# Decoding float64 weights on chip: two VectorE steps instead of three, in a kernel of linear attention and an expert layer

## The chip, the cores and the metric

One core of one Trainium2 chip runs the kernel. The metric is the device time of one execution in microseconds (us); the time of the kernel before is the median of three runs. The engines are TensorE (PE in the profile, with PEld for its weight loads), VectorE (DVE), ScalarE (ACT), GpSimd (POOL) and the DMA queue of SyncE (SP).

## What is computed

Linear attention over 8 batches of 8 heads, 576 tokens and 64 channels, followed by a layer with a SoLU (h times its softmax) and a normalisation. All inputs are drawn with numpy; the weights `w_in` and `w_out` of the second part reach the kernel as 64-bit floats, seen as pairs of 32-bit words.

```python
def phi(x):
    proj = np.einsum('bhsd,df->bhsf', x, w_phi)
    proj = proj - np.max(np.abs(proj), axis=-1, keepdims=True)
    return np.concatenate([np.exp(proj), np.exp(-proj)], axis=-1)
...
num = np.einsum('bhsf,bhfd->bhsd', q_p, kv)
den = np.einsum('bhsf,bhf->bhs', q_p, z)[..., None] + 1e-06
...
h = x @ w_in                               # 4608 x 512 times 512 x 1024
solu = h * softmax(h)
ln = (solu - mu) / np.sqrt(var + 1e-06) * g_ln
return (ln @ w_out).astype(np.float32)     # 4608 x 1024 times 1024 x 512
```

## The kernel before

**Staging.** Attention runs in 16 units (two per batch), each in two halves. A unit's keys are projected by TensorE (`kp`), VectorE takes each token's largest absolute value (`km`) and subtracts it (`ks`), ScalarE takes the exponentials (`ke`), and TensorE sums keys times values (`V`). The queries of the first three units go the same way (`qp`, `qm`, `qs`, transposes `qT` by TensorE, exponentials `qe`); later ones are turned by VectorE (`qt`, `qm4`, `qb`) and lessened by GpSimd (`qs`). TensorE multiplies the two (`qo`, or inside `V`), ScalarE takes the result out of PSUM (`qv`, `de`), VectorE and GpSimd divide (`dc`, `dv`), VectorE turns it (`xt`), and SyncE stores it to a scratch in DRAM (`xo`). The second part reads it back in 18 groups of two tiles of 128 tokens (`xi`), as products of a high and a low part in three matmuls each, with shared sums and differences (`as`, `xh`, `xl`, `h`, `kc`, `mx`), then the exponentials, the product, the centring, the turn through DRAM (`ex`, `u`, `cen`, `tb`, `bo`, `bi`), and the product with `w_out` (`o`).

**The weights.** `w_in` and `w_out` are loaded in eight pieces of 1 MB (`wl`, 0 to 3 of `w_in`, 4 to 7 of `w_out`), 128 partitions by 1024 numbers of two words. A number is decoded in four instructions: ScalarE multiplies the high word, taken as a 32-bit float, by 2^-112, which moves the exponent from the 64-bit to the 32-bit bias (`ws`, `w_rebias`); VectorE shifts it left by 3 (`wb` 0), puts the top three bits of the low word in (`wb` 1), and puts the sign back in, which the shift has pushed out (`wb` 2; all three in `w_bits`). In the profile they are `w<-wraw` on DVE and `wraw<-wraw` on ACT. ScalarE and GpSimd then make the high and low parts (`wh`, `wth`, `woh`; `wlo`, `wk`, `wtl`, `wol`); `W_IN_READY` holds the first product of the second part until all of `w_in` is there.

**What sets the order.** Every operation is registered with `op(...)`, with its engine, the operations that it comes after and the buffers that it takes and gives back; costs and priorities in the registration play no part at run time. The order is the list `SEQUENCE` of 2612 numbers, written out by hand: `Plan.order` walks it and gives each operation its buffer, and `InOrder` keeps each engine's instructions in that order. So an instruction that waits holds up all that stand behind it on its engine. The tag `h` of PSUM (two banks, 1024 columns) has one buffer, used by the second part for h; the tag `a` has six.

Of the kernel before, what the change touches and what calls it, by code (L numbers as in the profile page):

```python
# [8 lines left out]
F32 = mybir.dt.float32  # L9
F32R = mybir.dt.float32r  # L10
U32 = mybir.dt.uint32
# [7 lines left out]
DM, DF = 512, 1024  # L19
# [12 lines left out]
JOIN = 4  # L32
GROUPS = ((0, 4), (4, 1), (5, 4))
# [158 lines left out]
)  # L192


# [1121 lines left out]
```

## Time and profile before

| | |
|---|---|
| median of 3 runs | 658.42 us (657.59 to 659.11) |
| the profiled execution | 657.98 us |
| its span, from the first to the last instruction | 656.3 us |
| mean granted TensorE clock | 0.99 |
| busy, share of the span | PE 95%, DVE 75%, ACT 70%, POOL 66% |

The shares are averages over the span. The page also cuts the span into 40 slices, names the chain of work that ended last, and lists groups of instructions; a helper (`InOrder`) issues all of them, so that nearly every instruction has the same line, L274, and groups are told apart by the names of their tiles. A stretch of the trace can be asked for by itself: how busy each engine was, who waited for whom, and each instruction in order of time.

### The profile page before, as it was taken

Reading aid. Unit: us, or ns where it says so; the run is one execution under the profiler, and the core shown is the slowest. Engines: PE = TensorE matmul, PEld = TensorE weight load, DVE = VectorE, ACT = ScalarE, POOL = GpSimd, SP = SyncE. Lnnn points to the kernel's source line nnn. Section 1 sums busy time; section 2 is a strip of 40 time slices with the busy share of each in tenths; the row PEclk is TensorE's granted clock in tenths of the full one; section 3 lists DMA queues with packets and bytes.
Section 4 is the critical chain, followed back from the end, with each engine's and each line's share of the span. In section 5 each row is a group of like instructions: output and inputs, shape, how many; then the busy total and the mean of one; then the engine's idle time right before and its main releaser. Section 6 shows DMA issues by size and latency. Waiting matters only on the chain.

```text
span 656.3 us, 19000 instructions
## 1 busy us (share of the span) xinstructions
PE 625.5 (95%) x7558; PEld 528.0 (80%) x7558; DVE 489.6 (75%) x1003; ACT 458.8 (70%) x842; POOL 434.9 (66%) x468
## 2 busy tenths in 40 slices
PE   5879799999999999999999999999998999999998
PEld 4769687878887888888888887888886888778787
DVE  6999989778878778588786778998886773542740
ACT  3869689858875877478685666887783776465653
POOL 0468889788376875665967658748758556587642
PEclk9989899999999999999999999999998999999999
DMA  8955415472556553554545473646444443275432
GB/s 287 364 201 155 103 63 190 132 223 92 171 190 196 141 156 131 160 165 113 175 151 167 149 191 106 207 132 214 120 144 131 141 120 136 61 193 161 160 129 80
DMA packets 100200, 103.38 MB, mean 158 GB/s; under 512 B 50448, under 2 KB 73232, under 8 KB 99600
## 3 DMA queue, kind: packets, MB, share of 16 engines
q1 hardware_dynamic: 100112, 102.18, 50.5%
q8 instruction: 59, 0.97, 0.6%
q14 instruction: 29, 0.24, 0.1%
HBM read 64.92 MB, written 37.22 MB: 156 GB/s over the span
## 4 chain that ended last, share of the span: by engine, by line
PE 78%; DVE 9%; DMA 4%; POOL 3%; SPq 3%; issue 2%; ACT 1%; ACTq 0%; POOLq 0%; DVEq 0%
PE o L274 26%; PE U L274 12%; PE h L274 10%; PE kv L274 10%; PE num L274 10%; PE pjk L274 5%; PE pq L274 3%; SPq L274 3%; DVE w L274 2%; DVE m L274 2%; DMA wraw<-in_w_in 2%; DMA rv<-in_v 1%; DVE blk L274 1%; POOL w_out_l L274 1%; DVE ek L274 1%
## 5 line engine op out<-in xcount | busy, mean ns | idle before, releaser
L274 POOL TENSOR_TENSOR uls<-uTs,uhs 128x1024 fp32r<-128x1024 f32 x35 | 83.5, 2388 | 47.1 <-ACT uhs L274 31.3
L274 PE MATMUL o<-w_out_h,uhs 128*128 128x512 f32 x280 | 112.0, 400 | 0.0
L274 PE MATMUL o<-w_out_h,uls 128*128 128x512 f32 x280 | 109.4, 391 | 1.1 <-POOL uls L274 1.1
L274 PE MATMUL o<-w_out_l,uhs 128*128 128x512 f32 x280 | 109.3, 390 | 0.0
L274 ACT ACTIVATE ek<-ek 128x512 f32<-128x512 f32 (+1 forms) x160 | 90.8, 586 | 22.8 <-DVE ek L274 21.9
L274 ACT ACTIVATE fq<-fq 128x640 f32<-128x640 f32 (+1 forms) x104 | 69.8, 680 | 12.3 <-DVE fq L274 11.5
L274 PEld LDWEIGHTS num<-kvf,fq 128*64 128x64 f32 x2304 | 70.3, 138 | 9.4 <-issue 5.6
L274 PE MATMUL kv<-rv,ek 128*64 128x65 f32 x2048 | 77.5, 223 | 0.0
L274 PE MATMUL num<-kvf,fq 128*64 128x65 f32 x2304 | 74.8, 223 | 0.7 <-ACT fq L274 0.6
L274 PEld LDWEIGHTS kv<-rv,ek 128*64 128x64 f32 x2048 | 71.7, 139 | 0.7 <-issue 0.4
L274 POOL TENSOR_TENSOR al<-S,ah 128x512 fp32r<-128x512 f32 x36 | 47.9, 1331 | 32.6 <-ACT ah L274 28.0
L274 POOL TENSOR_TENSOR blk<-blk,m 128x1152 f32<-128x1152 f32 x26 | 55.5, 2136 | 20.8 <-DVE m L274 19.7
L274 POOL TENSOR_TENSOR y<-E,rc 128x512 f32<-128x512 f32 x64 | 43.4, 699 | 38.5 <-DVE rc L274 17.4
L274 ACT ACTIVATE eu<-h,nm 128x1024 f32<-128x1024 f32 x36 | 40.1, 1115 | 39.6 <-DVE nm L274 33.5
L274 DVE SCALAR_TENSOR_TENSOR eu<-h,eu 128x1024 f32<-128x1024 f32 x36 | 43.8, 1217 | 26.5 <-ACT eu L274 26.3
L274 PEld LDWEIGHTS o<-w_out_h,uls 128*128 128x128 f32 x280 | 52.6, 188 | 13.2 <-POOL uls L274 2.0
L274 PEld LDWEIGHTS o<-w_out_h,uhs 128*128 128x128 f32 x280 | 52.6, 188 | 12.5 <-issue 0.4
L274 PEld LDWEIGHTS o<-w_out_l,uhs 128*128 128x128 f32 x280 | 52.6, 188 | 10.4
L274 DVE TENSOR_REDUCE m<-pjk 128x4 f32<-128x512 f32 (+1 forms) x80 | 48.4, 620 | 10.4 <-PE pjk L274 10.0
L274 DVE STREAM_TRANSPOSE ub<-eu 128x1024 f32<-128x1024 f32 x35 | 43.1, 1230 | 17.3 <-ACT eu L274 5.7
L274 PE MATMUL pjk<-wph,rawk 64*128 64x128 f32 (+1 forms) x544 | 48.0, 292 | 5.0 <-DMA rawk<-in_k 2.0
L274 DVE TENSOR_TENSOR ek<-pjk,m 128x512 f32<-128x512 f32 (+1 forms) x80 | 48.9, 621 | 4.8 <-PE kv L274 3.9
(111 smaller groups left out, 1565.2 us busy)
## 6 DMA issues: line engine op xcount, KB each, us to landing
du<-ub SPq DMA_DIRECT2D x35, 512.0 KB, 3.0
uTs<-du SPq DMA_DIRECT2D x140, 128.0 KB, 3.0
dx<-y SPq DMA_DIRECT2D x32, 288.0 KB, 2.3
out<-os SPq DMA_DIRECT2D x35, 256.0 KB, 3.2
rv<-in_v SPq DMA_DIRECT2D x32, 264.0 KB, 3.9
rawk<-in_k SPq DMA_DIRECT2D x32, 256.0 KB, 4.0
xT<-dx SPq DMA_DIRECT2D x64, 128.0 KB, 3.6
rawq<-in_q SPq DMA_DIRECT2D x26, 288.0 KB, 3.3
```

The source lines that it names most:

```text
L274: return self.tc.keep_in_program_order(method(*args, **kwargs))
```

## The change

The decoding of a piece is three instructions instead of four. ScalarE multiplies by Prelu instead of Copy: a negative result is multiplied by another 2^32, which sets the bit of the exponent that a shift by 3 moves to the place of the sign. For the four pieces of `w_in` (`BY_PSUM`) the result goes to PSUM, into the one buffer of the tag `h`, instead of back to the loaded tile. VectorE's first step takes the top three bits of the low word, and needs only the load; the second shifts the rescaled word and joins the two. The sign step is gone. In the diff's names: `ws`, then `wb` and `wd` (w_in) or `wj` (w_out).

```diff
+BY_PSUM = (0, 1, 2, 3)
...
 SEQUENCE = (
-    128, 3, 129, 132, 133, 185, 188, 118, 130, 84, 95, 119, 23, 189, 131, 103, 122, 120, 86, 85, 91, 124, 24,
...
     def w_rebias(i):
 
-        hf = W["raw", i][:, :, 1].bitcast(F32)
-        nc.scalar.activation(out=hf, in_=hf, func=AF.Copy, scale=(-1.0 if i < 4 else 1.0) * 2.0**-112)
-
-    def w_bits(i, step, tag):
-        raw = W["raw", i]
-        lo, hi = raw[:, :, 0], raw[:, :, 1]
-        if step == 0:
-            W[i] = sb(tag, [P, DF], U32, f"w32_{i}")
-            nc.vector.tensor_scalar(out=W[i], in0=hi, scalar1=3, scalar2=None, op0=ALU.logical_shift_left)
-        elif step == 1:
-            nc.vector.scalar_tensor_tensor(
-                out=W[i], in0=lo, scalar=29, in1=W[i], op0=ALU.logical_shift_right, op1=ALU.bitwise_or
-            )
-        else:
-            nc.vector.scalar_tensor_tensor(
-                out=W[i], in0=hi, scalar=0x80000000, in1=W[i], op0=ALU.bitwise_and, op1=ALU.bitwise_or
-            )
+        hi = W["raw", i][:, :, 1].bitcast(F32)
+        W["hi", i] = hf = bank("h", [P, DF], "whi") if i in BY_PSUM else hi
+        nc.scalar.activation(
+            out=hf, in_=hi, func=AF.Prelu, scale=(-1.0 if i < 4 else 1.0) * 2.0**-112, alpha=2.0**32
+        )
+
+    def w_low_bits(i, tag):
+        W[i] = sb(tag, [P, DF], U32, f"w32_{i}")
+        nc.vector.tensor_scalar(
+            out=W[i], in0=W["raw", i][:, :, 0], scalar1=29, scalar2=None, op0=ALU.logical_shift_right
+        )
+
+    def w_join_bits(i):
+        nc.vector.scalar_tensor_tensor(
+            out=W[i], in0=W["hi", i].bitcast(U32), scalar=3, in1=W[i], op0=ALU.logical_shift_left, op1=ALU.bitwise_or
+        )
...
+    JOINED = [("wd", i) if i in BY_PSUM else ("wj", i, "wb") for i in range(8)]
...
         op(("wl", i), "sync", dma(8 * P * DF), z - 9, w_load, (i, None))
-        op(("ws", i), "scalar", 1055, z, w_rebias, (i,), [("wl", i)])
-        op(("wb", i, 0), "vector", 600, z, w_bits, (i, 0, w_tag[i]), [("ws", i)], [(w_tag[i], T)])
-        op(("wb", i, 1), "vector", 1135, z, w_bits, (i, 1, None), [("wb", i, 0)], tiles=[T])
-        op(("wb", i, 2), "vector", 1135, z, w_bits, (i, 2, None), [("wb", i, 1)], tiles=[T])
+        ps_ = i in BY_PSUM
+        op(("ws", i), "scalar", act(DF, True) if ps_ else 1055, z, w_rebias, (i,), [("wl", i)],
+           [("h", ("whi", i))] if ps_ else ())
+        op(("wb", i), "vector", 600, z, w_low_bits, (i, w_tag[i]), [("wl", i)], [(w_tag[i], T)])
+        op(("wd", i) if ps_ else ("wj", i, "wb"), "vector", 1135, z, w_join_bits, (i,), [("wb", i), ("ws", i)],
+           tiles=[T, ("whi", i)] if ps_ else [T])
```

The operations that came after the third step now come after the join (`JOINED`). The list `SEQUENCE` is new from end to end, with 2604 numbers. Translated into names, its beginning reads so:

- On VectorE the first decoding step stood behind 13 other instructions of the attention, and now stands behind 21. The order there was: first step of piece 3, of 1, second and third of 1, second of 3, first of 0, third of 3, second of 0, first of 2, third of 0, second of 2, third of 2, with other instructions between most of them. It is now: first step of 3, one subtraction, join 3, first step of 1, one reduction, join 1, three others, first step of 0, join 0, seven others, first step of 2, two others, join 2; much later the first step of 6, then both of 4, the first steps of 5 and 7, and the joins of 7, 6 and 5.
- On ScalarE the rescaling of piece 3 is third, with the exponentials of the first keys behind it; that of 1 stands behind the first unit's first queries, and that of 0 and 2 soon after.
- On GpSimd the first work on weights is the low part of piece 3 instead of a difference of piece 1.
- On SyncE the load of piece 1 stands four places later than before, and pieces 0 and 2 no longer directly behind each other.
- On TensorE the order of projections, transposes and products is nearly that of before, with swaps of neighbours. In the second part the second half of the first tile's h (`h` 1) mostly comes ahead of the fourth shared product (`u4`) now.

## Rows read from the trace of the kernel before

**Rows 1.** The page: busy time, share of the span and instructions of each engine; then TensorE's busy tenths and the granted clock in 40 equal slices of the span.
```profile
PE 625.5 (95%) x7558; PEld 528.0 (80%) x7558; DVE 489.6 (75%) x1003; ACT 458.8 (70%) x842; POOL 434.9 (66%) x468
...
PE   5879799999999999999999999999998999999998
...
PEclk9989899999999999999999999999998999999999
```

**Rows 2.** Busy time by stage: stretch and length, then busy us and instructions of PE, PEld, DVE, ACT and POOL, the granted clock, the DMA share and GB/s.
```profile
0.00:10.00 10.00, 6.20 (x52) 5.07 (x52) 4.05 (x8) 1.28 (x1) 1.25 (x9) 1.00 0.75 213
10.00:100.00 90.00, 74.18 (x1311) 63.51 (x1310) 84.81 (x125) 70.75 (x151) 60.53 (x42) 0.94 0.57 194
...
120.00:656.30 536.30, 526.24 (x5967) 443.46 (x5965) 381.13 (x831) 367.20 (x657) 354.45 (x402) 1.00 0.50 150
```

**Rows 3.** The same for the instructions that read or write the loaded words (`wraw`) alone: DVE, then ACT.
```profile
10.00:100.00 90.00, 36.53 (x24) 9.41 (x8) 0.94 0.57 194
```

**Rows 4.** The instructions on the tile `wraw`: ns at least, median and at most, first and last start in us, forms.
```profile
L274 DVE SCALAR_TENSOR_TENSOR w<-wraw,w x16: 1166/1222/3274, 18.3 to 91.9; 128x1024 uint32<-128x1024 uint32 x16
L274 ACT ACTIVATE wraw<-wraw x8: 1128/1168/1257, 11.4 to 66.7; 128x1024 f32<-128x1024 f32 x8
L274 DVE TENSOR_SCALAR w<-wraw x8: 677/1321/2405, 13.6 to 77.4; 128x1024 uint32<-128x1024 uint32 x8
```

**Rows 5.** Who TensorE waited for in the first 160 us: us in total, times, longest.
```profile
PE dT L274 <- DVE dq L274: 4.4, 3, 3.0
...
PE pjq L274 <- issue: 2.2, 1, 2.2
PE pjk L274 <- DMA rawk<-in_k: 2.0, 1, 2.0
...
PE pjk L274 <- DVE dq L274: 1.3, 1, 1.3
```

**Rows 6.** The chain of work that ended last, in order of time, in the first 200 us: start, us, what.
```profile
26.88 1.21 DVE w L274
...
42.05 1.96 PE pjk L274 x16
...
64.71 0.69 DVE m L274
...
78.69 0.90 PE dT L274 x3
79.59 2.69 PE U L274 x6
...
87.29 2.14 POOL blk L274
...
96.20 2.35 POOL w_out_l L274
```

**Rows 7.** VectorE's instructions in order of time, the decoding steps with two sources and one with one source: start, us, instruction, count.
```profile
25.75 2.35 DVE L274 SCALAR_TENSOR_TENSOR w<-wraw,w 128x1024 uint32<-128x1024 uint32 x2
...
28.62 2.40 DVE L274 TENSOR_SCALAR w<-wraw 128x1024 uint32<-128x1024 uint32 x1
30.95 2.29 DVE L274 SCALAR_TENSOR_TENSOR w<-wraw,w 128x1024 uint32<-128x1024 uint32 x1
...
34.36 1.96 DVE L274 SCALAR_TENSOR_TENSOR w<-wraw,w 128x1024 uint32<-128x1024 uint32 x1
...
39.35 2.05 DVE L274 SCALAR_TENSOR_TENSOR w<-wraw,w 128x1024 uint32<-128x1024 uint32 x1
...
67.35 2.37 DVE L274 SCALAR_TENSOR_TENSOR w<-wraw,w 128x1024 uint32<-128x1024 uint32 x1
...
70.67 3.27 DVE L274 SCALAR_TENSOR_TENSOR w<-wraw,w 128x1024 uint32<-128x1024 uint32 x1
...
75.06 1.77 DVE L274 SCALAR_TENSOR_TENSOR w<-wraw,w 128x1024 uint32<-128x1024 uint32 x1
```

**Rows 8.** GpSimd's instructions in order of time: start, us, instruction, count, in brackets the idle time before and what ended it.
```profile
21.06 2.19 POOL L274 TENSOR_TENSOR w<-w 128x512 f32<-128x512 f32 x1 [19.21 <-DVE w L274]
...
39.05 1.27 POOL L274 TENSOR_TENSOR w<-w 128x512 f32<-128x512 f32 x1
40.28 2.25 POOL L274 TENSOR_TENSOR w<-w,w 128x512 f32<-128x512 f32 x1
...
70.48 2.38 POOL L274 TENSOR_TENSOR wt_l<-w,wt_h 128x1024 fp32r<-128x1024 f32 x1 [1.85 <-ACT wt_h L274]
```

**Rows 9.** Groups of instructions of the first 120 us, shapes kept apart: count, busy us, mean ns, idle before and what ended it.
```profile
L274 DVE SCALAR_TENSOR_TENSOR w<-wraw,w 128x1024 uint32<-128x1024 uint32 x16 | 26.0, 1642 | 0.0
...
L274 DVE SCALAR_TENSOR_TENSOR eu<-h,eu 128x1024 f32<-128x1024 f32 x3 | 3.7, 1220 | 0.5 <-ACT eu L274 0.4
...
L274 ACT CAST wb_h<-w 128x1024 fp32r<-128x1024 f32 x2 | 2.1, 1044 | 1.3 <-DVE w L274 1.3
...
L274 ACT ACT_TABLE_LOAD x1 | 1.3, 1283 | 0.7 <-PEq L1306 0.7
```

**Rows 10.** Busy time by stage, columns as in rows 2, for two more stretches.
```profile
40.00:60.00 20.00, 18.71 (x375) 17.03 (x375) 19.21 (x32) 17.94 (x41) 15.84 (x13) 0.91 0.54 171
...
480.00:520.00 40.00, 37.18 (x540) 31.57 (x540) 30.24 (x67) 26.27 (x50) 26.74 (x28) 0.96 0.46 145
```

**Rows 11.** Who TensorE waited for behind 160 us: us in total, times, longest.
```profile
PE h L274 <- DVE nm L274: 3.7, 2, 2.8
```

More of the change, by code (lines that the diff above doesn't have):

```diff
@@ L485, in linear_attention_then_moe @@
         op(("wl", i), "sync", dma(8 * P * DF), z - 9, w_load, (i, None))
-        op(("ws", i), "scalar", 1055, z, w_rebias, (i,), [("wl", i)])
-        op(("wb", i, 0), "vector", 600, z, w_bits, (i, 0, w_tag[i]), [("ws", i)], [(w_tag[i], T)])
-        op(("wb", i, 1), "vector", 1135, z, w_bits, (i, 1, None), [("wb", i, 0)], tiles=[T])
-        op(("wb", i, 2), "vector", 1135, z, w_bits, (i, 2, None), [("wb", i, 1)], tiles=[T])
+        ps_ = i in BY_PSUM
[4 more added lines that the diff above has]
+           tiles=[T, ("whi", i)] if ps_ else [T])
         if i >= 4:
-            op(("wg", i), "scalar", 1260, z, w_gain, (i,), [("wb", i, 2), "gain"], tiles=[T])
+            op(("wg", i), "scalar", 1260, z, w_gain, (i,), [JOINED[i], "gain"], tiles=[T])
     for p in range(2):
@@ L494, in linear_attention_then_moe @@
         z = w_time[p + 2]
-        op(("wh", p), "scalar", 560, z, w_in_hi, (p, p), [("wb", p, 2)], tiles=[A])
+        op(("wh", p), "scalar", 560, z, w_in_hi, (p, p), [JOINED[p]], tiles=[A])
         op(("wlo", p), "gpsimd", 1225, z, w_in_lo, (p, p), [("wh", p)], tiles=[A])
-        op(("wh", p + 2), "scalar", 947, z, w_in_hi, (p, p + 2), [("wb", p + 2, 2)], tiles=[B_])
+        op(("wh", p + 2), "scalar", 947, z, w_in_hi, (p, p + 2), [JOINED[p + 2]], tiles=[B_])
         op(("wlo", p + 2), "gpsimd", 2303, z, w_in_lo, (p, p + 2), [("wh", p + 2)], tiles=[B_])
-        op(("wk", p, 0), "gpsimd", 1225, z + 1, w_comb, (p, 0), [("wb", p, 2)], tiles=[A])
+        op(("wk", p, 0), "gpsimd", 1225, z + 1, w_comb, (p, 0), [JOINED[p]], tiles=[A])
         op(("wk", p, 1), "gpsimd", 1225, z + 1, w_comb, (p, 1), [("wk", p, 0), ("wlo", p + 2)], tiles=[A, B_])
@@ L512, in linear_attention_then_moe @@
         first, second = 4 + 2 * ((i - 4) // 2), 5 + 2 * ((i - 4) // 2)
-        op(("woh", i), "scalar", 947, z, w_out_hi, (i,), [("wg", i), ("wb", first, 2)], tiles=[T])
-        op(("wol", i), "gpsimd", 2303, z, w_out_lo, (i,), [("woh", i), ("wb", second, 2)], tiles=[T])
+        op(("woh", i), "scalar", 947, z, w_out_hi, (i,), [("wg", i), JOINED[first]], tiles=[T])
+        op(("wol", i), "gpsimd", 2303, z, w_out_lo, (i,), [("woh", i), JOINED[second]], tiles=[T])
     def span(g):
```

272 rows, old and new, of the table SEQUENCE are left out of this document.

## The prediction

> **What bounds the kernel now.** I read the page first, then the same numbers cut into stages, then who TensorE waited for, then the chain that ended last, and at last the decoding instructions one by one. The reader should see four things.
>
> TensorE is the engine that ends last: it is busy 625.5 of 656.3 us, and its row of slices is full except at the start [rows 1]. The stages say where the other 30.8 us lie: from 120 us on it idles 10.1 us of 536, but between 10 and 100 us 15.8 us of 90 (90 - 74.18), and there the granted clock averages 0.94, which takes another 0.06 x 90 = 5.4 us of its work [rows 2]. So a change of the weights, which are decoded in this stretch alone, can win at most 15.8 + 5.4 = 21.2 us, and what comes later can only keep it or lose it.
>
> In the same stretch VectorE is busy 84.81 of 90 us [rows 2], and the 24 decoding instructions are 36.53 us of that [rows 3]. TensorE's waits name it: its transposes and projections wait 4.4 and 1.3 us for VectorE's subtraction `dq`; 2.0 us are a load of keys and 2.2 us nothing that the profile names [rows 5]. The chain goes the same way: from 26.88 to 42.05 us and from 64.71 to 78.69 us it is VectorE's queue, with decoding steps between the reductions that TensorE needs; from 87.29 to 98.55 us it is POOL [rows 6].
>
> The decoding steps have very different lengths: a step with two SBUF sources takes 1.17 us at least, 3.27 at most and 1.64 on average (26.0 us for 16, from the row of the page's first 120 us); the one-source step takes 0.68 to 2.41 us [rows 4, 9]. The long ones lie beside POOL's instructions: the step of 3.27 us at 70.67 beside one of POOL's from 70.48 [rows 7, 8]. POOL suffers too: the same 512-column subtraction takes 1.27 us alone and 2.19 or 2.25 us beside decoding steps [rows 8].
>
> **The change part by part.** The times are set against the profiled execution: 657.98 us, of which 656.3 are the span; it stands 0.44 us below the median of 658.42.
>
> *The third step goes.* Eight of 16 two-source steps vanish. Bare, that is worth 8 x 1.17 = 9.4 us of VectorE, at the mean 8 x 1.64 = 13.1 us. On the chain stand seven such steps: in the first stretch the second half of the pair at 25.75 (1.2) and those of 2.29, 1.96 and 2.05; in the second 2.37, 3.27 and 1.77 [rows 7]. They sum to 14.9 us, and half of that goes: **-7.5 us**. Bounds: 7 x 1.17 / 2 = -4.1 if only bare time is won, and -13.1 if all eight count. I take the middle value because it is read from the places where the chain ran.
>
> *The join of w_in reads PSUM.* Four of the eight remaining joins get one SBUF and one PSUM source. The trace has that form with the same 1024 columns: the product `eu<-h,eu` takes 1.22 us and hardly varies [rows 9]. Two such joins stand where the first stretch had steps averaging (1.2 + 2.29 + 1.96 + 2.05) / 4 = 1.88 us: 2 x 0.66 = **-1.3 us**; bounds 0 (no contention there any more anyway) and 4 x (1.64 - 1.22) = -1.7.
>
> The sources of the old steps are every second word, the PSUM source is dense. The rows show no price for the stride: 1.17 us at least with it, 1.22 in the dense form [rows 4, 9]. [...]
>
> *The rescaling.* Prelu in place of Copy, for w_in into PSUM. ScalarE's eight rescalings take 9.41 us together [rows 3], 1.17 us each [rows 4]; a dense 1024-column cast takes 1.04 us [rows 9]. 0 to -1.0 us of ScalarE, which is not the one that is late here (70.75 of 90 us [rows 2]): nothing. No row shows Prelu; the other functions share one table load in the whole span [rows 9]. If it doesn't, see the rivals.
>
> *The low word first.* The first step no longer waits for the rescaling, only for the load. VectorE had no idle time before any of these steps (the pieces follow without a gap [rows 7]), so nothing is won by itself: 0.
>
> *One PSUM buffer for four rescaled words.* The tag `h` has one slot. The rescaling of weight 1 waits for the join of weight 3, and by the new list only the first step of 1 and one reduction stand on VectorE between join 3 and join 1: 0.68 + 0.68 us against a rescaling of 1.17 us and two handovers. Behind that join waits all of VectorE, and behind the rescaling ScalarE's exponentials. I take **+0.5 us**; bounds 0 and 3 x 1.17 = +3.5 for three handovers. The list puts four and ten other instructions between the later joins, so the low end is nearer.
>
> *The clock.* TensorE's granted clock falls in this stage after it has waited for VectorE (its longest such wait is 3.0 us [rows 5]). If the first of these gaps closes, a part comes back: 40 to 60 us shows a granted 0.91, so 0.09 x 20 = 1.8 us [rows 10]; I take **-1.7 us**, bounds 0 and -5.4.
>
> *What is late next: POOL.* It begins its weights at 21.06 us [rows 8] and is busy 60.53 us between 10 and 100 [rows 2], so behind its start it has 90 - 11.1 - 60.5 = 18.4 us of idle time left to give. The new list puts weight 3 first, behind 21 reductions and subtractions of VectorE where 13 stood, so POOL starts no earlier. To end 8 us sooner it has to give up nearly half of its idle time. Bounds 0 and +8 (its chain at 87 us doesn't move at all); I take **+2.0 us**, nearer to the low end because its waits were for VectorE in the first place.
>
> *The new order of the rest.* TensorE's order of its products and of the attention changes only by swaps of neighbours; the second half of a tile's h now comes ahead of the fourth shared product. From 120 us on there are 10.1 us of idle time [rows 2], which can shrink or grow; I take 0.
>
> Sum: -7.5 - 1.3 + 0.5 - 1.7 + 2.0 = -8.0 us, so 657.98 - 8.0 = 650.0 for such an execution and **650.4 us** as a median.
>
> **The rivals.**
>
> *All of it arrives* (chance 0.15). The eight steps count at their mean, 13.1, and the four joins 1.7; less 0.5 that is 14.3, below the 21.2 - 2.0 - 2.2 = 17.0 us that TensorE can give back without its waits for keys and the nameless one. For it: VectorE is busy 94% of the stretch [rows 2]. Against it: between the two stretches of VectorE, from 42.05 to 64.71 us, the chain is TensorE's own work [rows 6], and an earlier start of it helps only as far as its inputs are there. Time 658.42 - 14.3 = 644.1.
>
> *POOL becomes the bound* (0.14). Its chain up to 98.55 us [rows 6] carries products and low parts that the change doesn't touch. Then only what POOL itself gains is left: two subtractions back from 2.19 and 2.25 to 1.27, 1.9 us. For it: 11.3 us of chain; against it: 18.4 us of idle time ahead of that. Time 656.5.
>
> *Slower: the new list opens gaps where TensorE is full* (0.12). The place is after 120 us, the mechanism a product of TensorE that stands too early behind VectorE's minimum `nm`. One such place exists: between 480 and 520 us TensorE stands still for 2.8 us [rows 11], and the stretch has a granted 0.96 over 40 us [rows 10], 1.6 us more: 4.4 us. One list trades such places for others; two more eat 8.8 us, so from the second on the gain is gone, and with three the time is 658.42 - 8.0 + 13.2 = 663.6. Against it: VectorE has slack there (381 of 536 us [rows 2]).
>
> *Slower too: Prelu needs another table* (0.03). The change then doesn't do what it says. Eight rescalings among exponentials mean up to 16 loads of 1.283 us [rows 9], 20.5 us of ScalarE, which with 70.75 [rows 2] would fill 91 us of the 82 that the forecast leaves for the stretch. The time lies between 650.4 + 9.3 and 650.4 + 20.5; I put 665. [...]
>
> **How the numbers follow.** The forecast has 0.56. The likeliest case reaches by its own bounds from 645 to 656. To hold 8 in 10 the range takes in most of the first rival and all of the second: 643.5 to 659.0, leaving out the slower rivals (0.15) and the lowest few. A measurement can tell about 0.2% from no change, 1.3 us here. Faster: the forecast (0.54 of its 0.56), the first rival 0.15 and half of the second, 0.08: 0.77. Same: 0.08. Slower: 0.15.
>
> **What would show it.** Right: 16 decoding instructions of some 20 to 24 us in all; joins of w_in at 1.2 us without long ones; TensorE's idle time between 10 and 100 us down by about 6 us; one table load. Wrong: TensorE's waits for `dq` replaced by equal ones for ScalarE or POOL (the PSUM slot, POOL's chain); more than 10 us of idle time after 120 us; more table loads. If the decoding shrinks as said but the first product of the expert network starts no earlier than at 79.59 us [rows 6], the step that took VectorE's saving for TensorE's was wrong.

## The result, and the profile after

The changed kernel takes 635.07 us, median of 4 runs (634.44 to 636.38), against 658.00 for the kernel before beside it: ratio 0.9657 [0.9629, 0.9685]. That is 15 us below the forecast of 650.4 and 8 below the low end of its range. The profiled execution took 634.97 us, its span 633.2.

The page of the kernel after: busy time by engine, TensorE's busy tenths, the granted clock, and the shares of the chain.

```profile
PE 617.8 (98%) x7558; PEld 525.0 (83%) x7558; DVE 475.3 (75%) x995; ACT 458.1 (72%) x842; POOL 432.0 (68%) x468
...
PE   6999899999999999999999999999999999999997
...
PEclk9999999999999999999999999999999999999999
...
PE 88%; DVE 6%; ACT 2%; DMA 2%; issue 1%; SPq 0%; ACTq 0%; DVEq 0%
```

TensorE idles 633.2 - 617.8 = 15.4 us instead of 30.8 [rows 1], and the row of the clock has no 8 left. (Read in steps of 1 us, the granted clock of the kernel before is 1.00 but for three places, 42 to 46, 76 to 84 and 499 to 504 us, each with 0.50 inside; a product of `h` takes 0.63 us at 501 us and 0.39 at 89 us. So its 0.96 between 480 and 520 us [rows 10] is a mean over a few us at 0.50 and the rest at 1.00. The kernel after has 1.00 in every such step.) The stages of the kernel after, with the columns of rows 2:

```profile
10.00:100.00 90.00, 83.83 (x1518) 72.43 (x1520) 83.78 (x142) 82.22 (x172) 69.55 (x50) 1.00 0.65 215
120.00:633.20 513.20, 508.24 (x5746) 430.86 (x5745) 371.54 (x810) 357.78 (x637) 345.36 (x394) 1.00 0.51 152
480.00:520.00 40.00, 39.40 (x571) 33.70 (x571) 34.56 (x77) 28.07 (x54) 26.31 (x33) 1.00 0.47 138
```

Between 10 and 100 us TensorE idles 6.2 us instead of 15.8, 9.6 us less, where the forecast's sign of being right asked for about 6. But behind 120 us it idles 5.0 us instead of 10.1 [rows 2], and the stretch from 480 to 520, where it stood still for 2.8 us at a granted 0.96 [rows 10], idles 0.6 us at 1.00 (the kernel after is at later work by then). VectorE is still busy 83.8 of the 90 us: a third step less did not make it idle, it made the stretch do more.

The decoding steps, first through PSUM, then the others; columns as in rows 4.

```profile
L274 ACT ACTIVATE whi<-wraw x4: 1074/1123/1131, 10.7 to 27.2; 128x1024 f32<-128x1024 f32 x4
L274 DVE SCALAR_TENSOR_TENSOR w<-whi,w x4: 1155/1219/1225, 18.4 to 32.6; 128x1024 uint32<-128x1024 uint32 x4
```

```profile
L274 DVE TENSOR_SCALAR w<-wraw x8: 682/1254/1739, 17.5 to 64.5; 128x1024 uint32<-128x1024 uint32 x8
...
L274 DVE SCALAR_TENSOR_TENSOR w<-wraw,w x4: 1714/1922/2106, 52.4 to 70.8; 128x1024 uint32<-128x1024 uint32 x4
```

The sums of the two, busy us of DVE and ACT between 10 and 100 us (the first row for the steps on loaded words, the second for those on PSUM):

```profile
10.00:100.00 90.00, 16.98 (x12) 9.30 (x8) 1.00 0.65 215
```

```profile
10.00:100.00 90.00, 4.82 (x4) 4.45 (x4) 1.00 0.65 215
```

16.98 + 4.82 = 21.8 us on VectorE against 36.53 [rows 3]; the forecast said 20 to 24. Who TensorE waits for, in the first 160 us and behind them:

```profile
PE pjq L274 <- DMA wph<-in_w_phi: 3.8, 1, 3.8
PE U L274 <- DVE blk L274: 2.2, 1, 2.2
PE h L274 <- DVE nm L274: 1.0, 1, 1.0
PE pjk L274 <- DMA rawk<-in_k: 0.9, 1, 0.9
PE pjq L274 <- DVE dq L274: 0.7, 1, 0.7
```

```profile
PE pq L274 <- DVE c L274: 0.6, 1, 0.6
PE pq L274 <- ACT os L274: 0.2, 1, 0.2
```

The 4.4 and 1.3 us for `dq` [rows 5] have shrunk to three waits of 0.4 to 0.7 us, a new wait of 2.2 us for VectorE's turn `blk` has come, and the 3.7 us for `nm` behind 160 us [rows 11] are gone altogether. One piece of the chain:

```profile
68.40 1.62 PE U L274 x6
```

The first product of the second part starts at 68.40 us instead of 79.59 [rows 6]. GpSimd's first work on weights starts at 22.09 us, 1 us later than before [rows 8]; there is one table load, 1.3 us, as in rows 9.

```profile
22.09 2.38 POOL L274 TENSOR_TENSOR wb_l<-w,wb_h 128x1024 fp32r<-128x1024 f32 x1 [20.24 <-DVE w L274]
```

```profile
L274 ACT ACT_TABLE_LOAD x1 | 1.3, 1283 | 0.7 <-PEq L1308 0.7
```

**A landmark.** To tell the head from the rest in every kernel, I use the first product with `w_out`: it needs the weights of both kinds and all of the first tile's chain. Its start is the first number behind the durations in the row of `o<-w_out_h,uhs`, here for the kernels before and after:

```profile
L274 PE MATMUL o<-w_out_h,uhs x280: 387/389/586, 115.8 to 649.3; 128*128 128x512 f32 x140
```

```profile
L274 PE MATMUL o<-w_out_h,uhs x280: 387/389/587, 102.2 to 626.3; 128*128 128x512 f32 x140
```

So the head took 115.8 us and takes 102.2, 13.6 less; from there to the end of the span it was 656.3 - 115.8 = 540.5 and is 633.2 - 102.2 = 531.0, 9.5 less. The landmark is not quite the same place in both: the new list has one projection of TensorE ahead of it (16 products of unit 4's keys, `kp` 2, some 1.1 us) that the old list has behind it. Counted on the same side the head wins 14.7 us and the rest 8.4. More than a third of the gain lies where the forecast put nothing.

### The profile page after: what moved, and what is told of

Its sections match the earlier page's. It is cut to its first block, busy times and chain, and to the rows that moved or that the text cites. A ratio compares the mean times of both kernels' runs of the same rounds, so it can differ in the third digit from the quotient of the medians.

```text
span 633.2 us, 19010 instructions
## 1 busy us (share of the span) xinstructions
PE 617.8 (98%) x7558; PEld 525.0 (83%) x7558; DVE 475.3 (75%) x995; ACT 458.1 (72%) x842; POOL 432.0 (68%) x468
## 4 chain that ended last, share of the span: by engine, by line
PE 88%; DVE 6%; ACT 2%; DMA 2%; issue 1%; SPq 0%; ACTq 0%; DVEq 0%
PE o L274 31%; PE U L274 15%; PE h L274 12%; PE num L274 10%; PE kv L274 9%; PE pjk L274 5%; PE pq L274 4%; DVE m L274 2%; DVE w L274 1%; DVE ek L274 1%; PE pjq L274 1%; DVE dq L274 1%; DMA xT<-dx 1%; ACT fq L274 1%; DMA out<-os 1%
## 5 line engine op out<-in xcount | busy, mean ns | idle before, releaser
L274 PEld LDWEIGHTS o<-w_out_h,uhs 128*128 128x128 f32 x280 | 52.6, 188 | 12.5 <-issue 0.2
L274 POOL TENSOR_TENSOR al<-S,ah 128x512 fp32r<-128x512 f32 x36 | 47.5, 1320 | 21.8 <-ACT ah L274 20.9
L274 DVE STREAM_TRANSPOSE ub<-eu 128x1024 f32<-128x1024 f32 x35 | 43.1, 1233 | 14.3 <-ACT eu L274 5.5
L274 DVE STREAM_TRANSPOSE blk<-pq 128x320 f32<-128x320 f32 (+1 forms) x104 | 43.4, 455 | 10.8 <-PE pq L274 10.7
L274 POOL TENSOR_TENSOR lq<-rawq,hq 128x576 fp32r<-128x576 f32 x26 | 37.2, 1432 | 20.9 <-ACT hq L274 20.1
```

What stands on the lines that cost most here:

```text
L274: return self.tc.keep_in_program_order(method(*args, **kwargs))
```

## The experiments

All with the landmark read in the same way from each kernel's own row. The ratio is to the kernel before on the same chip.

| kernel | median us | ratio, 95% | span | head | rest |
|---|---|---|---|---|---|
| before | 658.0 | | 656.3 | 115.8 | 540.5 |
| e1 new decoding, no PSUM, old list | 648.78 | 0.9867 [0.9841, 0.9893] | 648.9 | 108.1 | 540.8 |
| e2 old decoding, new list | 648.35 | 0.9878 [0.9845, 0.9910] | 645.7 | 114.5 | 531.2 |
| e3 new without PSUM | 638.43 | 0.9711 [0.9690, 0.9733] | 636.8 | 104.8 | 532.0 |
| e4 new head, old rest | 643.64 | 0.9790 [0.9769, 0.9812] | 641.7 | 102.2 | 539.5 |
| e5 e1 with the new rest | 642.67 | 0.9756 [0.9720, 0.9792] | 641.9 | 107.9 | 534.0 |
| e6 before, one join moved | 653.30 | 0.9929 [0.9902, 0.9955] | 651.9 | 116.2 | 535.7 |
| e7 before, clock held | 656.80 | 0.9980 [0.9964, 0.9997] | 653.4 | 115.4 | 538.0 |
| e8 e3, high word first | 640.21 | 0.9727 [0.9687, 0.9767] | 640.6 | 107.4 | 533.2 |
| e9 after, one stretch old | 644.92 | 0.9809 [0.9784, 0.9835] | 644.2 | 103.8 | 540.4 |
| e10 after, joins of w_in twice | 641.54 | 0.9751 [0.9725, 0.9777] | 641.6 | 108.3 | 533.3 |
| e11 after, joins of w_out twice | 642.89 | 0.9767 [0.9743, 0.9792] | 638.2 | 107.3 | 530.9 |
| e12 after, four operations moved | 638.05 | 0.9694 [0.9670, 0.9718] | 636.7 | 103.2 | 533.5 |
| e13 e4, one join moved | 640.81 | 0.9740 [0.9721, 0.9758] | 639.9 | 104.3 | 535.6 |
| e14 after, two more joins by PSUM | 635.67 | 0.9672 [0.9653, 0.9691] | 633.2 | 100.9 | 532.3 |
| e15 after, beside e13 and e14 | 635.80 | 0.9668 [0.9651, 0.9686] | 633.5 | 101.9 | 531.6 |

Kernels with one and the same list behind the head (e3, e8, e10, e11, e14, e15) show rests of 530.9 to 533.3, so a single span tells rests apart to some 2 us; the medians are the judge below that. The same holds for heads: the kernel after, e9 and e15 have one code and one order up to the landmark, and heads of 101.9 to 103.8. All kernels with the new list at their beginning (e2 to e4 and e8 to e15, and the kernel after) have the 1.1 us of projection in the head.

**Decoding and list apart: e1, e2, e3.** The names in the list stand for the numbers.

```diff
# e1: the list before
-BY_PSUM = (0, 1, 2, 3)
+BY_PSUM = ()
-SEQUENCE: new
+SEQUENCE: that of before, each join at the place of its second step, third steps struck
# e2: the kernel before, SEQUENCE new (three steps: the second and third at the place of the join)
# e3: only BY_PSUM = ()
```

> The kernel before, with its own list, but with two decoding steps: the join stands where the second step stood, the third is struck out, and the rescaled words of w_in stay in the loaded tile (the old list has no room for the PSUM buffer). Theory D (the decoding does it: VectorE's 14.7 us less decoding between 10 and 100 us bring back TensorE's idle time and the clock there, 14.9 us): 643 to 647 us. Theory O (the list does it; the two steps are worth only what the old chain shows, about 8 us, because the old list leaves no place for more): 648 to 654 us.

> The kernel before with its three decoding steps, in the new list: the second and third step stand one behind the other where the join stands. Theory D: VectorE gets its 14.7 us back, so the head is as late as before, and only what the list saves behind 100 us is left: 648 to 652 us. Theory O: the list keeps most of its gain: 637 to 644 us.

> The changed kernel with the rescaled words of w_in back in the loaded tile; list and two steps unchanged. Both theories: the four joins of w_in meet GpSimd again, 4 x (1.64 - 1.22) = 1.7 us of VectorE: 635 to 638 us. If the PSUM operand is the main thing, it is 640 us or more, with joins of 2 us and longer among those of w_in.

By the ratios each half alone is worth 8 to 9 us (e1 and e2), both together without PSUM 19 (e3), and with it 23. By the landmark the halves lie in different places: e1 shortens the head by 7.7 us and leaves the rest (540.5, 540.8); e2 leaves the head nearly alone (1.3 us) and shortens the rest by 9.3. The rest does not care how the weights were decoded. In the head, the new list is worth 1.3 us with the old decoding (115.8 to 114.5) and 3.3 with the new (e1 to e3, 108.1 to 104.8), each with 1.1 us more work of TensorE in it. What e1 waited for in its head and e3 and the kernel after don't (they have instead 2.2 us for `blk`):

```profile
PE U L271 <- POOL al L271: 1.8, 1, 1.8
PE h L271 <- DVE nm L271: 1.6, 2, 1.1
```

The order of the loads may be a part of it too. The chain of the kernel before [rows 6] begins with loads, up to 26.86 us, the longest a piece of `w_in`:

```profile
12.78 10.85 DMA wraw<-in_w_in
```

e7, with the old list, has that load on its chain as well (9.63 us); the chains of e2 and of the kernel after, with the new list, have no load of `w_in` or `w_out` ahead of the landmark. What this alone is worth no run tells.

e3 against the kernel after tells PSUM's share: 3.4 us by the medians, 3.6 by the ratios, whose intervals leave anything from 0.3 to 7. e3's four joins of w_in, from SBUF, on VectorE in order of time:

```profile
18.16 1.22 DVE L274 SCALAR_TENSOR_TENSOR w<-wraw,w 128x1024 uint32<-128x1024 uint32 x1
...
20.59 1.23 DVE L274 SCALAR_TENSOR_TENSOR w<-wraw,w 128x1024 uint32<-128x1024 uint32 x1
...
24.88 2.12 DVE L274 SCALAR_TENSOR_TENSOR w<-wraw,w 128x1024 uint32<-128x1024 uint32 x1
...
33.21 1.51 DVE L274 SCALAR_TENSOR_TENSOR w<-wraw,w 128x1024 uint32<-128x1024 uint32 x1
```

They sum to 6.08 us against 4.82 after: 1.26 us of VectorE, nearly the forecast's 1.3. The joins at 18.16 and 20.59, before GpSimd has work (21.84 us in e3), take as long from SBUF as from PSUM; only the two later ones are long. Beyond that, e3 has a granted clock of 0.98 between 10 and 100 us where the kernel after has 1.00, which is 0.02 x 90 = 1.8 us; the two make 3.1 of the 3.4. But that clock is not shown to be PSUM's: e13, whose joins do read PSUM, has the same lower clock in the same place, behind a wait of 2.1 us for `blk` where e3 has one of 2.2. From 70 to 80 us, first e3, then e13:

```profile
70.00:80.00 10.00, 10.00 (x42) 8.00 (x40) 7.92 (x15) 7.42 (x18) 9.82 (x8) 0.84 0.29 79
```

```profile
70.00:80.00 10.00, 10.00 (x44) 7.89 (x44) 7.86 (x16) 7.27 (x17) 9.85 (x7) 0.84 0.27 77
```

The kernel after has the same wait and 1.00 there.

**Where the list wins: e4, e5.** Spliced lists: the order of one list up to a point, and behind it what is left in the order of the other.

```diff
# e4: the kernel after
-SEQUENCE: new
+SEQUENCE: the first 500 places of the new one (about 100 us), the rest in the old order
# e5: e1
-SEQUENCE: old
+SEQUENCE: the first 888 places of the old one (about 205 us), the rest in the new order
```

> The changed kernel, whose list follows the new one for its first 500 operations (to about 100 us) and takes the rest in the order of the old list. Theory D and theory O both put about 15 us (idle time and clock) into the head; the rest of the new list then brings 23 - 15 = 8 us, and without it the time is 642 to 645 us. If the list behind the head is worth nothing by itself, and an earlier head alone closes the later gaps, it is 634 to 637 us.

> Two decoding steps without the PSUM buffer; the list follows the old one for its first 888 operations (to about 205 us) and the new one behind that. If what the new list saves behind the head is a thing of its own and adds up: 648.8 - 8.6 = 640 us, with TensorE's waits for nm behind 205 us gone. If the gaps behind the head come from a late head: 646 to 649 us.

e4 keeps the head to the tenth (102.2) and loses 8.5 us in the rest, 8.6 by the medians, which agrees with the 8.4 above; e5 keeps the head of e1 and wins 6.1 by the medians, 7.3 by the ratios, with the new order from 205 us on. So the list's gain is real, lies behind the head, and most of it behind 205 us.

**One operation: e6, e9, e13.** The 2.8 us of rows 11 are a wait of TensorE for the join `mx` 0 of group 11. In the list before it stands on VectorE behind reductions of unit 15, whose projections TensorE makes just before, and TensorE's next `h` stands behind the join.

```diff
# e6: the kernel before; e13: e4
+ ("moe", 11, "mx", 0)   directly behind ("moe", 11, "kc", 2), ahead of unit 15's reductions
- ("moe", 11, "mx", 0)   ahead of ("moe", 11, "h", 1)
# e9: the kernel after, its places 2060 to 2149 sorted into the order of the list before
```

> The kernel before with one operation of its list moved: the first minimum of group 11 (mx 0), at 498.7 us of VectorE, from behind the reductions of unit 15 to just behind the group's second kept sum, so that TensorE's product at 499.5 us no longer waits for it. If that wait is the list's own and drags the clock: -2.8 us for the wait and -1.7 to -3.6 us for the half-speed stretch behind it, 651 to 653.5 us. If the gap only moves on to the next wait: 656 to 658 us.

> The kernel after, with 90 of its 2604 places, those about group 11 near 470 to 490 us, put back into the order of the list before: the join of the first half of h (mx 0, which ends in the minimum nm) again stands on VectorE behind the two reductions of unit 15, whose projections TensorE makes just before, and the second half of h waits for it. Theory (one badly placed operation is most of what the list is worth behind the head): the wait of 2.8 us of rows 11 and the stretch of lower clock behind it (0.04 x 40 = 1.6 us, rows 10) return in the new list too: 635.1 + 4.4 = 639.5. Rival (the list's gain is spread over many small places, and 90 of 2604 places are worth little): 635 to 636. Rival (only the wait returns, without the clock): 637.9.

> The kernel with the new head and the old rest (643.6 us, 8.6 above the kernel after), with one operation of the rest moved: the join of the first half of group 11's h stands directly behind the third shared difference of its group on VectorE, ahead of the reductions of unit 15. Theory (one place holds most of it: a wait of 2.8 us and the lower clock behind it, as in the same move in the kernel before, which won 4.8): 643.6 - 4.8 = 638.8, and 3.8 us are left for all other places together. Rival (the old rest waits elsewhere once this wait is gone): 642 to 643.6. Rival (it is the whole): 635.

Moving that one operation wins (1 - 0.9929) x 658 = 4.7 us; the forecast had priced such a place at 4.4. The stretch of e6 with columns as in rows 10:

```profile
480.00:520.00 40.00, 40.00 (x608) 34.44 (x607) 33.12 (x73) 28.72 (x54) 30.48 (x32) 1.00 0.56 169
```

Putting 90 of 2604 places back (e9) costs 9.8 us, twice what was expected and more than the list wins behind the head; it opens a second gap too. Its VectorE queue shows how such a wait is built:

```profile
482.85 0.78 DVE L271 STREAM_TRANSPOSE blk<-pq 128x256 f32<-128x256 f32 x2 [0.33 <-PE pq L271]
483.56 0.23 DVE L271 RECIPROCAL rc<-rc 128x18 f32<-128x18 f32 x1
483.70 1.22 DVE L271 TENSOR_REDUCE m<-pjk 128x4 f32<-128x512 f32 x2
484.84 0.69 DVE L271 CUSTOM_DVE_ANT_0 h<-h,c 128x512 f32<-128x512 f32 x1
```

and TensorE's side of it, with the second gap, which lies behind the end of the old stretch:

```profile
485.64 0.75 PE L271 MATMUL h<-wb_h,ah 128*128 128x512 f32 x1 [2.82 <-DVE nm L271]
498.33 0.50 PE L271 MATMUL h<-wt_h,ah 128*128 128x512 f32 x1 [2.70 <-DVE nm L271]
```

Two gaps of 5.5 us, and a granted clock behind them that takes more:

```profile
460.00:520.00 60.00, 54.48 (x674) 45.49 (x673) 44.77 (x102) 36.03 (x67) 35.52 (x39) 0.94 0.35 105
```

0.06 x 60 = 3.6 us. As the kernel after idles 0.6 us in that stretch, this makes 4.9 + 3.6 = 8.5 of the 9.4 by which e9's rest is longer. In the kernel after, whose list has TensorE's `h` ahead of the join, VectorE has this wait instead, and TensorE has no gap there:

```profile
479.60 0.70 DVE L274 CUSTOM_DVE_ANT_0 h<-h,c 128x512 f32<-128x512 f32 x1 [3.98 <-PE h L274]
```

e13 tells how much of the 8.5 us is this one place: its rest is 3.9 us shorter than e4's, with 460 to 520 us full at 1.00 in place of 57.18 us busy at 0.97 in e4. The median fell by 2.8 only (3.3 by the ratios); in the profiled executions e13's head has a granted 0.98 where e4's has 1.00, 1.8 us, which would make up the difference. Of e13:

```profile
10.00:100.00 90.00, 82.60 (x1446) 71.21 (x1447) 81.60 (x138) 79.81 (x168) 67.31 (x50) 0.98 0.64 210
...
460.00:520.00 60.00, 60.00 (x713) 50.62 (x713) 49.53 (x115) 44.08 (x81) 41.71 (x44) 1.00 0.45 139
```

So between a third (by the medians) and nearly half (by the rests) of the rest's gain is one place, and 535.6 - 531.0 = 4.6 us are spread over small ones. Four waits of e13 behind 160 us that the kernel after doesn't have sum to 2.8 us, against 0.8 of its own there:

```profile
PE o L271 <- POOL uls L271: 1.2, 2, 0.8
PE h L271 <- DVE nm L271: 0.9, 1, 0.9
PE pjk L271 <- DVE blk L271: 0.4, 1, 0.4
PE pq L271 <- DVE fq L271: 0.3, 1, 0.3
```

**The clock by itself: e7.** Idle fill products in the gaps of the head, into a buffer that is free there. Products of their size, 128 x 128, stand in the kernel before as the transposes `dT`: at a granted 1.00 two of them take 0.44 us (at 20.96 us) and twelve 1.53 (at 48.35 us).

```diff
+def fill(n):
+    w = bank("h", [P, 512], "fill")
+    for _ in range(n):
+        nc.tensor.matmul(w[:, :P], lhsT=ident, rhs=ident, start=True, stop=True)
# 5, 5, 5 and 12 of them, ahead of four products of units 1 and 2
```

> The kernel before with 27 idle matmuls (128 x 128, into the unused PSUM tag h, 0.22 us each at full speed) in four places of TensorE's queue where it waits: 5 each ahead of three operations at 34, 39.8 and 42 us and 12 ahead of the one at 77.5 us. They compute nothing that is used. If the half-speed stretches between 10 and 100 us cost what they show, 5.4 us: 652 to 654 us with a granted 1.00 there. If VectorE is the bound in that stretch anyway and a faster TensorE only waits longer: 656 to 659 us.

The time falls by 0.2% (0.9980 [0.9964, 0.9997]), 1.3 us. The granted clock is 1.00 throughout in three of the ten executions, the profiled one among them, and 0.991 to 0.997 in the others; those three take 655.14 to 655.79 us. In the profiled one, the shortest of the ten, the head ends only 0.4 us earlier (115.4), and the other 2.5 us lie behind it, where the stretch from 480 to 520 us has 1.00 instead of 0.96. So in the head the clock by itself is worth little: while VectorE is late, faster products only wait longer. It shows at the last of the four places, where a transpose waits for `dq`, first before, then in e7, where the fill products end just ahead of it:

```profile
77.49 0.90 PE L274 MATMUL dT<-ident,dq 128*128 128x128 f32 x3 [3.03 <-DVE dq L274]
```

```profile
77.55 0.54 PE L270 MATMUL dT<-ident,dq 128*128 128x128 f32 x3
```

It runs faster and starts no earlier.

**The order of the two words: e8.**

```diff
# on e3: high word first, low word in the join
-W = low >> 29                     # needs the load
-W = (high << 3) | W               # needs the rescaling
+W = high << 3                     # needs the rescaling
+W = (low >> 29) | W
```

> As e3 (two steps, new list, no PSUM buffer), but with the high word first: the first step shifts the rescaled word and waits for the rescaling, the second puts the low word in. The forecast said 0 for the order of the words: 637.5 to 639.5 us, as e3. If the early first step is what lets VectorE go on while ScalarE is late: waits of VectorE for ScalarE appear ahead of the first steps and the time is 640 us or more.

1.8 us more than e3, with intervals that overlap, so the time doesn't settle it. The profile shows a wait that e3 and the kernel after don't have, 3.0 us of VectorE in front of the first steps:

```profile
L274 DVE TENSOR_SCALAR w<-wraw 128x1024 uint32<-128x1024 uint32 x8 | 9.1, 1150 | 3.0 <-ACT wraw L274 3.0
```

**The price of VectorE's time: e10, e11.**

```diff
 def w_join_bits(i):
+    for _ in range(2 if i in (0, 1, 2, 3) else 1):     # e11: (4, 5, 6, 7)
+        w_join_once(i)
```

> The kernel after, with each of the four joins of w_in (PSUM source, 1.16 to 1.22 us each) done twice, which leaves the numbers as they are: 4 x 1.19 = 4.8 us more of VectorE in the first stretch. Theory (VectorE sets the pace of the head and all of its time there is on the path): 635.1 + 4.8 = 639.9, up to 641.6 if a stretch of lower clock comes with it. Rival (as forecast, half of a step's time is on the path): 637.5. Rival (POOL or the loads are late by now): 635 to 636.

> The kernel after, with each of the four joins of w_out (SBUF sources, 1.71 to 2.11 us beside POOL) done twice, which leaves the numbers as they are: 4 x 1.9 = 7.6 us more of VectorE between 60 and 85 us. Theory (all of VectorE's time in the head is on the path): 635.1 + 7.6 = 642.7. Rival (half of it, as forecast): 638.9. Rival (w_out has slack, because TensorE by then has the products of the first groups): 635 to 637.

The groups of the first 120 us that were doubled, first e10, then e11:

```profile
L274 DVE SCALAR_TENSOR_TENSOR w<-whi,w 128x1024 uint32<-128x1024 uint32 x8 | 9.7, 1215 | 0.7 <-ACT whi L274 0.5
```

```profile
L274 DVE SCALAR_TENSOR_TENSOR w<-wraw,w 128x1024 uint32<-128x1024 uint32 x8 | 13.4, 1675 | 0.2
```

e10 adds 9.7 - 4.8 = 4.9 us to VectorE and 6.1 to the head (6.5 to the median; its profiled execution, 643.34, is the longest of its six); e11 adds 13.4 - 7.7 = 5.7 to the joins and 5.1 to the head (7.8 to the median; its profiled execution, 639.97, is the shortest of its five). Both have a lower clock in these profiles (0.96 between 10 and 100 us). The two executions of e10 with a granted 1.00 take 638.89 and 639.36 us, 3.8 and 4.3 more than the kernel after, for 4.9 us of VectorE; the profiled one of e11 is 4.9 us longer for 5.7. So some four fifths of VectorE's time in the head is on the path, not half of it, and a lower clock comes on top.

**Two tries for more: e12, e14.**

```diff
# e12: on the kernel after, only VectorE's order
- first steps of 5 and 7, join of 7   ahead of unit 3's transposes
+ first steps of 5 and 7, join of 7   behind them
- turn of group 3                     ahead of group 2's join (mx 0)
+ turn of group 3                     behind it
# e14
-BY_PSUM = (0, 1, 2, 3)
+BY_PSUM = (0, 1, 2, 3, 4, 7)
```

> The kernel after, with four of VectorE's operations moved behind others in the list: the first decoding steps of pieces 5 and 7 and the join of 7 behind the two transposes of unit 3 for which TensorE's first product waits 2.15 us at 68.4 us, and the turn of group 3 behind the join of group 2's h for which TensorE waits 0.95 us at 135.4 us. Theory (each of TensorE's remaining waits for VectorE is one misplaced operation and can be closed by itself): up to 2.15 + 0.95 = 3.1 us less, less what GpSimd's parts allow (ready at 66.8 us, so 1.6 of the 2.15): 632.5. Rival (the head is bound by VectorE's whole queue, so the wait moves to the next operation): 634.1 from the second place alone, or 635.1 with neither.

> The kernel after, with pieces 4 and 7 of w_out rescaled into PSUM too, in the same order of all operations. Two joins read one SBUF and one PSUM source: 1.9 to 1.2 us, 1.4 us less of VectorE between 52 and 68 us. Theory (VectorE's time sets the pace of the head, at the price of 1.0 to 1.4 us for each that the doubled joins showed): 1.4 to 2.0 us less than the kernel after, 633.4. Rival (GpSimd's parts for the first products are ready at 66.8 us at the earliest and set the end of the head): no change, 635.1. Rival (the one PSUM buffer, which the first h takes next, is held longer by piece 7): 1 us more.

> The kernel after, unchanged, on the same chip as the two others, as the yardstick for differences of a few tenths of a per cent: 634.4 to 636.4 us.

e12 is no faster than the kernel after, rather 2.4 us slower (0.9694 against 0.9657, the intervals just overlap). The wait for `blk` at 68 us is gone, and TensorE waits for GpSimd's low parts instead, and 1.17 us for another `blk` at 120.77 us; the other gap keeps its length, because the difference ahead of the join now waits 1.30 us for ScalarE's `c`. Of e12:

```profile
71.49 0.50 PE L271 MATMUL U<-wt_h,al 128*128 128x512 f32 x1 [0.80 <-POOL al L271]
76.12 0.50 PE L271 MATMUL h<-wb_h,al 128*128 128x512 f32 x1 [1.57 <-POOL al L271]
...
137.90 0.47 PE L271 MATMUL h<-wb_h,ah 128*128 128x512 f32 x1 [0.95 <-DVE nm L271]
```

e14 stands level with the kernel after on the same chip (635.67 and 635.80). Its joins through PSUM are as short as hoped:

```profile
L271 DVE SCALAR_TENSOR_TENSOR w<-whi,w 128x1024 uint32<-128x1024 uint32 x6 | 7.2, 1208 | 0.7 <-ACT whi L271 0.5
L271 DVE SCALAR_TENSOR_TENSOR w<-wraw,w 128x1024 uint32<-128x1024 uint32 x2 | 3.4, 1686 | 0.0
```

7.2 + 3.4 = 10.6 us against 4.8 + 7.7 = 12.5 in the first profile after. Its head is 1.0 us shorter than e15's, and its rest 0.7 longer. Adding time to VectorE costs most of it, and taking 1.9 us more away gave nothing that can be measured. Whether that is the next wait, or the lower clock of e14's head (0.98 against e15's 1.00, 1.8 us), stays open. No kernel here beats the one after.

## Why the prediction was wrong

The forecast of -8.0 us became -23. By its own steps:

| step | forecast us | measured us | by |
|---|---|---|---|
| the third step goes | -7.5 | -7.7 in the head, -8.8 by the ratio (with Prelu and the low word first) | before, e1 |
| joins by PSUM, one buffer, rescaling | -1.3 + 0.5 + 0 | -3.4 (1.26 of it VectorE's own) | e3, after |
| the low word first | 0 | -1.8, not settled | e8, e3 |
| the clock of the head | -1.7 | by itself -0.4 in the head, -1.3 by the median | e7 |
| POOL late next | +2.0 | no wait for it | after |
| order of the head | no term | -3.3 (-1.3 with the old decoding) | e1, e3; e2 |
| the new order of the rest | 0 | -8.6 | e4, after |

These rows overlap a little (e1's gain and PSUM's hold some of the clock), so they are not to be summed to the tenth; the landmark is: 13.6 of head and 9.5 of rest, or 14.7 and 8.4 with the same work on both sides. The head alone would have given some 644 us, inside the range; the rest took the time out of it.

*The step that failed* is "From 120 us on there are 10.1 us of idle time [rows 2], which can shrink or grow; I take 0", and with it the sentence of the first part that what comes later "can only keep it or lose it". The mechanism was on the page: rows 11 show a single wait of 2.8 us and rows 10 the clock behind it, and the text priced them at 4.4 us. It used that price only for the rival in which the new list opens such gaps, never for the case that it closes the one that is there. e6 closed it alone in the old kernel and won 4.7 us; e9 reopened it in the new one, with a second; and without the new order of the rest (e4) the whole change loses 8.6 us. The list was new from end to end and the places around group 11 could be read in both: the second half of h stands behind the join in one and ahead of it in the other. A term of 0 between -11.7 (the 10.1 us of idle time [rows 2] and 1.6 of clock [rows 10]) and +8.8 should have stood in the range with both ends; the low end of 643.5 left the lower one out.

*The third step* was right in its size, and the mechanism held: seven steps on the chain, half of their 14.9 us; e1 gave 7.7 in the head. That half is not a rule, and that it fitted is in part luck. It belongs to the old order: in the new one the shorter decoding brings the head 9.7 us (114.5 in e2 to 104.8 in e3), and e10 and e11 show that VectorE's time there counts for some four fifths. This, with the order of the head, which had no term, is why the head won more than the forecast's 8.0.

*PSUM* was right in its term, 1.26 us of VectorE measured against 1.3. The time fell by 3.4, and where the other 2 us come from stays open: the lower clock of e3's head is one candidate, but e13 has it with PSUM too. Neither the one buffer nor the rescaling cost anything that TensorE's waits show.

The runs show no price for the stride either: joins of every second word take 1.22 and 1.23 us in e3 before GpSimd has work, joins of dense PSUM words 1.16 to 1.23 in the kernel after. What PSUM saves VectorE is the longer steps beside GpSimd: 2.12 and 1.51 us in e3, where the joins through PSUM take 1.22 and 1.16.

*POOL* began 1 us later, no earlier, as said, and still was not late: TensorE has no wait for it in the kernel after. e1, the new decoding in the old order, does wait 1.8 us for POOL's `al`, and so do e2, the old decoding in the new order (1.8), e4 (0.8) and e12 (0.8 and 1.6). So POOL is close behind, as the +2.0 said, and the decoding and the order of the head together keep most of its wait out; that order had no term in the sum. The 1.27 us that the forecast took for GpSimd's subtraction alone stand in rows 8 at 39.05 us, beside the decoding step of 39.35 [rows 7, 8]; the same 1.27 us stand at 42.49 us, where no decoding step runs. So not every subtraction beside a decoding step is longer.

*The rivals.* "All of it arrives" came nearest (644.1), and still held only the head: 13.6 us measured there, 14.7 with the same work, against its 14.3. Prelu brought no second table load: the kernel after has one of 1.28 us in its span, as the kernel before [rows 9].

What stays open: which small places make up the 4.6 us of the rest beside group 11, what PSUM is worth beyond VectorE's 1.26 us, and whether the low word first is worth anything. The clock doesn't follow the waits strictly either: e7 keeps the gap of 2.8 us, and its stretch from 480 to 520 us has a granted 1.00.

## What to carry to other kernels

When a hand-written order is replaced as a whole, price its waits in both directions: each long single wait of the bound engine in the trace of before is a gain that the new order may hold, and looking up that one place in both lists is minutes of work. Split a large change by a landmark that exists in both traces (here the first product with the last weights) before explaining any of it. An engine that is busy 93% of a stretch can cost most of its time when something is added, and give nothing when something is taken: in e12 the next wait stood only a us or two behind.

## What the runs showed of the hardware

VectorE's two-source steps on SBUF take 1.2 us while GpSimd is idle (e3: 1.22 and 1.23) and 1.5 to 2.1 beside it (e3: 1.51 and 2.12; the kernel after: 1.71 to 2.11; up to 3.27 before [rows 4]). Not every one is longer beside it: in the kernel before a step at 56.21 us takes 1.17 and a pair at 83.83 us 2.34, and there GpSimd's instructions are the longer ones (two `y` from 56.42 us 2.14 in place of 1.32, an `al` from 84.76 us 2.58 in place of 1.35). With one source in PSUM the steps take 1.22 and 1.16 us beside it too (the kernel after, at 25.12 and 32.62 us; six in e14 average 1.21). A lower granted clock came behind single waits of TensorE of 2 to 3 us in some executions, with 1.6 to 3.6 us of lost work (0.96 over 40 us in e4 and rows 10, 0.94 over 60 us behind two waits in e9), and closing the wait gave back both (e6: 480 to 520 us full at 1.00); in others the same waits left it at 1.00 (e7 with 2.8 us from 480 to 520, the kernel after with 2.2 ahead of 68.40 us). A Prelu of 1024 columns takes 1.07 to 1.13 us into PSUM, a little less than the 1.13 to 1.26 us of the Copy that it replaces in SBUF [rows 4]; the span has one table load of 1.28 us with it, as without it.
